# Pooled attention and a three-way maxout layer: more products by the seven-product scheme, and loads that wait for work ahead of them, in one written order

## The chip, the cores and the metric

The kernel runs on one core of a Trainium2 chip. The metric is the device time of one execution in microseconds (us); lower is better. TensorE is PE in the profile, its weight loads PEld, VectorE DVE, ScalarE ACT, GpSimd POOL, SyncE SP.

## The reference

```python
# q, k, v: (8, 8, 576, 64) float32: batch, heads, sequence, head size
k_p = k.reshape(B, H, 72, 8, D).mean(axis=3)       # keys and values pooled by 8
v_p = v.reshape(B, H, 72, 8, D).mean(axis=3)
scores = scale * np.matmul(q, k_p.transpose(0, 1, 3, 2))
attn = softmax(scores)
attn_out = np.matmul(attn, v_p)                    # (8, 8, 576, 64)
x = attn_out.transpose(0, 2, 1, 3).reshape(4608, 512)
h = np.maximum(np.maximum(x @ w1, x @ w2), x @ w3) # w1, w2, w3: (512, 768)
out = h @ w_out                                    # (768, 512)
```

## The kernel before

**Attention.** Eight batches, one after the other. Keys and values are loaded by POOL's queue as 16-bit numbers (load_k, load_v, load_q), 576 KB each, into two buffers a kind. The eight rows of a pool are added in three steps (fold_steps, L157 to L164): for batch 1 the keys on DVE, from batch 2 on keys and values on POOL. turn_k (L204) turns the pooled keys with TensorE and copies them with zeros into a block matrix kz; queries are turned by TensorE for batches 0 to 2 and by one DMA transpose on SP from batch 3 on (L302). scores (L227) gives a whole head at a time, 576 columns in two PSUM banks; from batch 7 on scores_flat (L234) gives pieces of 512 columns. ACT takes the exponential. values (L264) multiplies 128 tokens with the pooled values of eight heads and a column for the sum, DVE takes the reciprocal (rcp) and multiplies (xn). turn_x brings the tokens into xT, a ring of 2048 tokens with channels in partitions: by TensorE up to batch 2, by DMA transposes on SP (L253) from batch 3 on.

**Maxout.** With w2 - w1 and w3 - w1 in place of w2 and w3, the hidden layer is max(0, x(w2 - w1), x(w3 - w1)) plus x w1, and the output is that maximum times w_out plus x times wm, where wm = w1 w_out is made once (linear, L345). Tokens go in nine tiles of 512, numbered 0 to 8. An ordinary first layer (hidden, L362) takes 48 matmuls of 512 columns for a tile; an ordinary output (project, L412 and L416) takes 40 of 512 columns.

**Seven products.** A two by two block product can be made with seven block products instead of eight, when sums of the blocks are made first. The kernel uses this form with products named 1 to 7: PRODUCTS names the operands, S1 to S4 sums of the weight blocks and T1 to T4 sums of the token blocks. A first layer then takes 84 matmuls of 256 columns (seven, L789), an output 70 of 256 (out_seven, L713). Before, first layers of tiles 6, 7 and 8 are made so, and outputs of tiles 2, 3, 4, 7 and 8. Weight sums are made on DVE (fold_w L536, fold_out L597), token and hidden sums on DVE in tiles 2 to 4 (L612) and partly on POOL in tiles 6 to 8 (L564, L628).

**Order.** Every engine runs its instructions in the order in which the program gives them. Tile 0 and the start are run by block with a plan of steps in slots, tiles 1 to 4 by the lists in MIDDLE, tile 5 by LEAD, the rest by ORDER in weave. In MIDDLE a step such as `k5<` loads the keys of batch 5, and the key load waits for the last first-layer matmul issued before it; `!` makes the next POOL step wait for the last weight or token sum on DVE (gate). Stores of finished rows (osb, ob) go out on SP, 128 or 256 KB each.

Of the kernel before, what the change touches and what calls it, by code (L numbers as in the profile page):

```python
# [14 lines left out]
def kernel(  # L15
# [11 lines left out]
    nc = tc.nc  # L27
# [37 lines left out]
    kts, vts, qbs, kps, qTs, ets = {}, {}, {}, {}, {}, {}  # L65

# [15 lines left out]
    def load_v(b, eng, dtype=F16, cuts=(0, H)):  # L82
        if b == 0:
            vts[0] = ld.tile([96, 4096], dtype, name="vt0", tag="vt")[:, 0:3072].rearrange(
                "p (h i d) -> p h i d", h=H, i=6)
            src = v[0].rearrange("h (p i) d -> p h i d", i=6)
            return [eng.dma_start(out=vts[0][:, h:g], in_=src[:, h:g])
                    for h, g in zip(cuts, cuts[1:])][-1]
# [5 lines left out]
    def load_q(b):  # L94
# [4 lines left out]
        for i in range(0, 4, n):  # L99
            nc.gpsimd.dma_start(out=qbs[b][:, i:i + n], in_=src[:, i:i + n])  # L100
# [42 lines left out]
    vp_all = const.tile([Sp, B, H, 65], F16, name="vp", tag="vp")  # L143
# [10 lines left out]
    def fold(e, t, out, dtype=F32):  # L154
        return list(fold_steps(e, t, out, dtype))

    def fold_steps(e, t, out, dtype=F32):  # L157
        part, n = t.shape[:2]
        f = const.tile([part, n, 4, D], dtype, name="half" if dtype == F32 else "halfh",
                       tag="half" if dtype == F32 else "k16")  # L160
        yield e.tensor_tensor(out=f, in0=t[:, :, 0:4, :], in1=t[:, :, 4:8, :], op=ALU.add)  # L161
        yield e.tensor_tensor(out=f[:, :, 0:2, :], in0=f[:, :, 0:2, :],  # L162
                              in1=f[:, :, 2:4, :], op=ALU.add)
        yield e.tensor_tensor(out=out, in0=f[:, :, 0, :], in1=f[:, :, 1, :], op=ALU.add)  # L164

    def new_kp(b):
        kps[b] = sb2.tile([96, 6, D], BF16, name="kp", tag="kp")

    def fold_k(b, e, i0=0, i1=6):
        if b not in kps:  # L170
            new_kp(b)
        fold(e, kts[b][:, i0:i1], kps[b][:, i0:i1], F16 if e is nc.vector else F32)

    def fold_v(b):
        fold(nc.gpsimd, vts[b], vp_all[:, b, :, 0:D])

    def pool_v(b, h, g, tag, evac):

        pvp = psum([128, g - h, D], F32, name="pvp", tag=tag[0], bufs=tag[1])
        for i in range(6):  # L180
            nc.tensor.matmul(pvp, pick[:, i, :], vts[b][:, h:g, i, :],
                             start=(i == 0), stop=(i == 5))
        evac(out=vp_all[:, b, h:g, 0:D], in_=pvp[0:Sp])

    def turn_q(b, n0, n1, evac, tag):
# [5 lines left out]
        for n in range(n0, n1):  # L191
            nc.tensor.transpose(pqt[:, n - n0, :], qf[:, 128 * n:128 * n + 128],
                                ident)
        evac(out=qTs[b][:, n0:n1, :], in_=pqt)  # L194

    def keys(b, tag):
        pkt = psum([128, 3, 96], BF16, name="pkt", tag=tag[0], bufs=tag[1])
        for i in range(3):
            nc.tensor.transpose(pkt[:, i, :],
                                kps[b][:, 2 * i:2 * i + 2, :].rearrange("p i d -> p (i d)"),  # L200
                                ident[0:96, 0:96])
        return pkt

    def turn_k(b):  # L204
        pkt = keys(b, ATT if len(pools) < 3 else SC)
        for par, evac in enumerate((nc.vector.tensor_copy, nc.scalar.copy)):
            for odd in range(2):
                (evac if b > 2 else nc.vector.tensor_copy)(
# [4 lines left out]
    def score(b, h, out, tp, i0, i1):  # L213
# [4 lines left out]
        nc.tensor.matmul(out, kz_all[b % 2][f % 2][rows, h, :],  # L218
# [28 lines left out]
    def turn_x(b, c0, keep, xn, tag, evac=nc.scalar.copy):  # L247
        g0 = S * b + c0
        if b > 2:
            cut = 128 - (g0 + 128) % RING  # L250
            cuts = (keep, cut, 128) if keep < cut < 128 else (keep, 128)
            for a, z in zip(cuts, cuts[1:]):
                nc.sync.dma_start_transpose(  # L253
                    out=tokens(g0 + a, g0 + z),
                    in_=xn.rearrange("p g h d -> p (g h d)")[a:z])
            return
        pxt = psum([128, KCH, 128], F16, name="pxt", tag=tag[0], bufs=tag[1])
        for kc in range(KCH):
            nc.tensor.transpose(
# [4 lines left out]
    def values(b, c0):  # L264
        tag = (ATT0, ATT, ("val", 1))[len(pools) - 1]
        pav = psum([128, 2, 512], F32, name="pav", tag=tag[0], bufs=tag[1])
        for h in range(H):
            nc.tensor.matmul(  # L268
                pav[:, h // 4, 65 * (h % 4):65 * (h % 4) + 65],
                ets[b][:, h, c0:c0 + 128], vp_all[:, b, h, :],  # L270
# [18 lines left out]
    xns, mms = {}, []  # L289

    def do(b, steps):
# [3 lines left out]
        for name in steps.split():  # L295
            i = int(name[1:] or 0)
            if name[0] in "qQ":
                turn_q(b, *QS[i], nc.vector.tensor_copy if name[0] == "Q"
                       else nc.scalar.copy, TR)
# [680 lines left out]
```

## Time and profile before

| | us |
|---|---|
| median of three runs (lowest, highest) | 226.58 (226.14, 226.96) |
| the profiled execution | 228.01 |
| its span, first to last instruction | 226.3 |

| engine | busy us | share of the span | instructions |
|---|---|---|---|
| PE | 214.7 | 95% | 1807 |
| DVE | 148.6 | 66% | 292 |
| ACT | 122.3 | 54% | 221 |
| POOL | 138.6 | 61% | 111 |

The granted TensorE clock is 1.00 over the whole span. Busy times of DVE and ACT overlap where one instruction starts before the one ahead has ended, and a matmul's own duration runs past the start of the next one; work on TensorE is therefore better counted by the distance between two starts. The chain of waits names the work that ended last at each step; idle time of an engine that is not the bottleneck costs nothing.

### The profile page before, as it was taken

The page shows a single profiled execution, that of the slowest core. Times are in us where ns is not written, and L with a number is a line of the kernel's source. Part 1 is how long each engine was busy: PE and PEld are TensorE (multiplying, and loading weights), DVE is VectorE, ACT ScalarE, POOL GpSimd, SP SyncE. Part 2 cuts the span into 40 slices and gives each one's busy share as a digit, 9 for nine tenths or more (in the row PEclk, how much of TensorE's full clock was granted, in tenths as well). Part 3 has the DMA queues.
Part 4 walks back from the last instruction along what each step waited for, and adds up shares of the span by engine and source line. Part 5 has one row for each costly group of instructions (what it writes and reads, how often), then busy time and mean ns, then how long its engine had stood idle before and what let it go on. Part 6 is the DMA issues. An engine that isn't in the chain of part 4 may idle for free.

```text
span 226.3 us, 4691 instructions
## 1 busy us (share of the span) xinstructions
PE 214.7 (95%) x1807; PEld 146.4 (65%) x1807; DVE 148.6 (66%) x292; ACT 122.3 (54%) x221; POOL 138.6 (61%) x111
## 2 busy tenths in 40 slices
PE   6788999999999999999999999699999999999993
PEld 2467745558656555965686568355677677788882
DVE  3668876038595385876679668535668886898840
ACT  2267524755874577238624862475687446555330
POOL 7974300999949967787677758999500913872020
PEclk9999999999999999999999999999999999999999
DMA  6999999989759999659999599965241534200265
GB/s 167 210 197 197 208 207 208 203 163 224 128 106 191 217 220 208 112 129 151 199 226 191 31 216 236 182 126 132 58 107 29 122 61 95 46 3 0 55 203 164
DMA packets 47351, 33.54 MB, mean 148 GB/s; under 512 B 27041, under 2 KB 42337, under 8 KB 47329
## 3 DMA queue, kind: packets, MB, share of 16 engines
q0 software_dynamic: 16944, 16.98, 48.1%
q1 hardware_dynamic: 29936, 15.87, 33.0%
q10 hardware_dynamic: 448, 0.39, 0.7%
q8 instruction: 14, 0.23, 0.5%
q14 instruction: 9, 0.07, 0.1%
HBM read 34.60 MB, written 9.44 MB: 195 GB/s over the span
## 4 chain that ended last, share of the span: by engine, by line
PE 69%; DMA 15%; POOL 11%; issue 1%; DVE 1%; ACT 1%; POOLq 0%
PE pw L362 21%; PE oA L713 9%; DMA vt<-in_v_dram 8%; PE pA L789 7%; PE po L416 7%; PE po L412 5%; PE oC L713 4%; PE psc L218 4%; DMA mw<-in_moe_w_dram 4%; PE pC L789 3%; POOL half L161 3%; DMA xT<-xn 3%; PE pav L268 3%; PE oB L713 2%; POOL half L162 2%; PE pB L789 2%
## 5 line engine op out<-in xcount | busy, mean ns | idle before, releaser
L362 PE MATMUL pw<-xT,mw 128*128 128x512 f16 (+1 forms) x336 | 72.8, 348 | 1.9 <-DMA xT<-xn 1.6
L362 PEld LDWEIGHTS <-mw 128*128 128x128 f16 x336 | 31.6, 98 | 22.3 <-DMA xT<-xn 1.8
L370 DVE TENSOR_TENSOR hT<-t,pw 128x512 f16<-128x512 f16 (+1 forms) x42 | 25.4, 609 | 25.1 <-ACT et L223 17.8
L223 ACT ACTIVATE et<-psc 72x576 f16<-72x576 f32 (+2 forms) x54 | 35.2, 661 | 6.8 <-PE psc L218 6.7
L161 POOL TENSOR_TENSOR half<-vt 72x2048 f32<-72x2048 f16 x7 | 28.4, 4061 | 13.8 <-DMA vt<-in_v_dram 13.3
L162 POOL TENSOR_TENSOR half<-half 72x1024 f32<-72x1024 f32 (+1 forms) x13 | 27.3, 2098 | 11.0 <-DVE rcp L274 6.1
L368 ACT ACTIVATE t<-pw 128x512 f16<-128x512 f32 (+1 forms) x42 | 22.5, 537 | 16.2 <-PE pw L362 15.8
L276 DVE TENSOR_TENSOR xn<-pav,rcp 128x512 f16<-128x512 f32 x40 | 27.7, 692 | 1.4
L416 PE MATMUL po<-mwo,hT 128*128 128x512 f16 (+1 forms) x102 | 23.5, 366 | 0.0
L218 PE MATMUL psc<-qT,kz 128*128 128x320 bf16 (+2 forms) x120 | 22.4, 278 | 0.8 <-DVE qT L194 0.6
L218 PEld LDWEIGHTS <-kz 128*128 128x128 bf16 x143 | 13.1, 98 | 13.3 <-ACT qT L194 1.1
L161 POOL TENSOR_TENSOR half<-ktFalse 96x1536 f32<-96x1536 f16 x6 | 18.7, 3125 | 4.0 <-issue 2.9
L564 POOL TENSOR_TENSOR pad<-xT 128x256 f16<-128x256 f16 x8 | 5.9, 732 | 22.5 <-ACT pad L795 13.9
L795 ACT CAST pad<-pA 128x512 f16<-128x512 f32 x27 | 15.6, 588 | 7.2 <-PE pA L789 7.0
L268 PEld LDWEIGHTS <-et 72*128 72x128 f16 x320 | 15.1, 98 | 3.6 <-issue 0.4
L723 ACT COPY osb<-oA 128x512 f32<-128x512 f32 x12 | 7.0, 586 | 19.2 <-PE oA L713 19.2
L274 DVE RECIPROCAL rcp<-pav 128x8 f32<-128x8 f32 x40 | 8.2, 204 | 14.0 <-PE pav L268 13.6
L412 PE MATMUL po<-wm,xT 128*128 128x512 f16 (+1 forms) x68 | 16.6, 366 | 0.0
L268 PE MATMUL pav<-vp,et 72*128 72x65 f16 x320 | 16.4, 194 | 0.1
L421 ACT COPY osb<-po 128x512 f32<-128x512 f32 (+1 forms) x16 | 9.2, 573 | 12.0 <-PE po L416 12.0
L789 PEld LDWEIGHTS <-sw 128*128 128x128 f16 x144 | 13.7, 98 | 2.5
L766 DVE TENSOR_TENSOR pad<-pad,pC 128x512 f16<-128x512 f16 x18 | 12.3, 685 | 3.9 <-PE pC L789 3.6
(122 smaller groups left out, 380.0 us busy)
## 6 DMA issues: line engine op xcount, KB each, us to landing
out_dram<-osb SPq DMA_DIRECT2D x38, 128.0 KB, 5.5
ktFalse<-in_k_dram POOLq DMA_DIRECT2D x7, 576.0 KB, 8.2
qb<-in_q_dram POOLq DMA_DIRECT2D x7, 576.0 KB, 13.0
vt<-in_v_dram POOLq DMA_DIRECT2D x7, 576.0 KB, 17.5
mw<-in_moe_w_dram POOLq DMA_DIRECT2D x9, 256.0 KB, 9.4
out_dram<-osb SPq DMA_DIRECT2D x8, 256.0 KB, 7.4
ktTrue<-in_k_dram SPq DMA_DIRECT2D x3, 384.0 KB, 5.2
out_dram<-ob SPq DMA_DIRECT2D x8, 128.0 KB, 2.6
```

What stands on the lines that cost most here:

```text
L161: yield e.tensor_tensor(out=f, in0=t[:, :, 0:4, :], in1=t[:, :, 4:8, :], op=ALU.add)
L162: yield e.tensor_tensor(out=f[:, :, 0:2, :], in0=f[:, :, 0:2, :], in1=f[:, :, 2:4, :], op=ALU.add)
L218: nc.tensor.matmul(out, kz_all[b % 2][f % 2][rows, h, :], qTs[b][rows, n + i0:n + i1, 64 * (h % 2):64 * (h % 2) + 64], start=True, stop=True)
L223: nc.scalar.activation(out=out, in_=in_, func=FT.Exp, scale=1.0 / 64.0)
L268: nc.tensor.matmul(pav[:, h // 4, 65 * (h % 4):65 * (h % 4) + 65], ets[b][:, h, c0:c0 + 128], vp_all[:, b, h, :], start=True, stop=True)
L276: nc.vector.tensor_tensor(out=xn, in0=pv[:, :, :, 0:D], in1=rcp.to_broadcast([128, 2, 4, D]), op=ALU.mult)
L362: mm = nc.tensor.matmul(pw, w_sb[wi][:, kc, bass.ts(jc, 128)], x[:, kc], start=(kc == 0), stop=(kc == KCH - 1))
L370: nc.vector.tensor_tensor(out=hT[:, jc, c0:c1], in0=t, in1=pw, op=ALU.max)
L412: nc.tensor.matmul(po, tokens(128 * m, 128 * m + 128)[:, kc], wm_sb[:, kc, c], start=(kc == 0), stop=False)
L416: nc.tensor.matmul(po, hT[:, jc, bass.ts(mm, 128)], wo_sb[:, jc, c], start=False, stop=(jc == JCH - 1))
L713: nc.tensor.matmul(p, left, right, stop=(r == 4), skip_group_check=True, start=(i in FIRST and r == 0 and (m == 0 or n == LAST)))
L789: mm = nc.tensor.matmul(p[:, w], a[:, kc, bass.ts(g, 128)], b[:, kc, :], start=(i in FIRST and w + kc == 0), stop=(w + kc == 2), skip_grou ...
```

## The change

The start of the program, up to the first layer of tile 0 and the product wm, is the same. Behind it:

- Tile 5's first layer and the outputs of tiles 1, 5 and 6 are made by seven products too. Only tile 0's output is ordinary now (project), and tile 1's first layer is made in halves of 256 tokens.
- Product 1 is copied into the PSUM bank in which products 2 and 3 add up, so the sums with product 1 are made by TensorE. PSUM has four banks that are taken and given back in turn (take, give), two for scores and turns, and two for values.
- All scores from batch 1 on are scores_flat: 23 matmuls a batch instead of 16, and nine exponentials of 512 columns instead of eight of 576.
- The key sums go from POOL to DVE, in two steps instead of three; the third addition is made by TensorE, which turns both halves of the sum into one bank (keys). The copies of the turned keys are on ACT, but for batch 1. The value sums stay on POOL, in six pieces a batch (four of 512 columns, two of 512 columns); the last addition is on DVE.
- All weight, token and hidden sums are on DVE (both, sum_t, sum_h). Each value piece on POOL waits for the last of these sums that was issued before it.
- The query transposes on SP are made in three parts a batch. Every load waits for the last matmul issued before it and for the last DMA transpose issued before it.
- From tile 0's output on, one list (ORDER, run) gives the order of everything. `<k3` loads keys of batch 3, `K3` and `V3` are pieces of its sums, `k3` turns keys, `s30` to `s38` are scores, `v30` to `v34` values, `T3` transposes a third of the queries, `A1` to `H4` are ordinary first-layer products, `1a` to `7c` first-layer products of the seven, `1d` to `7d` output products, `t` and `u` sums of tokens and hidden rows, `f F S G` weight sums; a star puts the copy on DVE.

```diff
+    def matmul(*args, **kw):
+        latest[0] = nc.tensor.matmul(*args, **kw)
+        return latest[0]
...
+    def fold_k(b):
+        new_kp(b)
+        f = const.tile([96, 6, 4, D], F16, name="halfh", tag="k16")
+        nc.vector.tensor_tensor(out=f, in0=kts[b][:, :, 0:4, :], in1=kts[b][:, :, 4:8, :],
+                                op=ALU.add)
+        nc.vector.tensor_tensor(out=kps[b].rearrange("p j i d -> p i j d"), in0=f[:, :, 0:2, :], in1=f[:, :, 2:4, :],
+                                op=ALU.add)
...
         for i in range(3):
-            nc.tensor.transpose(pkt[:, i, :],
-                                kps[b][:, 2 * i:2 * i + 2, :].rearrange("p i d -> p (i d)"),
-                                ident[0:96, 0:96])
+            for j in range(2):
+                matmul(pkt[:, i, :], kps[b][:, j, 2 * i:2 * i + 2, :].rearrange("p i d -> p (i d)"),
+                                 identh[0:96, 0:96], start=(j == 0), stop=(j == 1))
...
-                qTs[b] = sb2.tile([128, 2 * NG, 128], BF16, name="qT", tag="qT")
-                nc.sync.dma_start_transpose(
-                    out=qTs[b], in_=qbs[b].rearrange("p hp t d -> p (hp t d)"))
+                if i == 0:
+                    qTs[b] = sb2.tile([128, 2 * NG, 128], BF16, name="qT", tag="qT")
+                turned[:] = [nc.sync.dma_start_transpose(
+                    out=qTs[b][:, 6 * i:6 * i + 6],
+                    in_=qbs[b].rearrange("p hp t d -> p (hp t d)")[:, 768 * i:768 * i + 768])]
...
+    def both(out, a, b, op, e=nc.vector):
+        t = e.tensor_tensor(out=out, in0=a, in1=b, op=op)
+        if e is nc.vector:
+            shared[:] = [t]
...
+    def sum_t(x, t, i):
+        a, b = ((x[1], x[0]), (x[3], t[:, 0]), (x[3], x[1]), (x[2], t[:, 1]))[i]
+        both(t[:, i], a, b, ALU.subtract)
...
+        if i == 1:
+            move(out=bank("B", n, g), in_=p)
+        elif i in (6, 5):
+            move(out=y[:, i == 5], in_=p)
+        elif i in (2, 3):
+            t0 = sb2.tile([128, NB], F16, name="t0", tag="t0")[:, 0:HALF]
+            nc.scalar.activation(out=t0, in_=p[:, 0], func=FT.Relu)
+            nc.vector.tensor_tensor(out=h_of(g)[:, i - 2], in0=t0, in1=p[:, 1], op=ALU.max)
...
+        for i in range(0, H, 2):
+            c = slice(i, i + 2)
+            yield e.tensor_tensor(out=f[:, c], in0=t[:, c, 0:4, :], in1=t[:, c, 4:8, :],
+                                  op=ALU.add)
+        for i in range(0, H, 4):
+            c = slice(i, i + 4)
+            yield e.tensor_tensor(out=t[:, c, 0:2, :], in0=f[:, c, 0:2, :], in1=f[:, c, 2:4, :],
+                                  op=ALU.add)
+        both(vp_all[:, b % 3, :, 0:D], t[:, :, 0, :], t[:, :, 1, :], ALU.add)
+        yield
+
+    def piece(what, b):
+        if (what, b) not in folding:
+            folding[what, b] = pieces(what, b)
+        gate = shared[0]
+        op = next(folding[what, b])
+        if op is not None and gate is not None:
+            after([op], gate)
...
+    SEVEN = (5, 6, 7, 8)
...
+            elif name[0] == "<":
+                load = {"k": load_k, "v": load_v, "q": load_q}[name[1]](
+                    int(name[2]), *([nc.gpsimd] if name[1] != "q" else []))
+                after([load], latest[0])
+                if turned:
+                    after([load], turned[0])
...
+    ORDER = """
+        V1 q12* q13 V1 p V1 V1 s10 s11 V1 p* <k3 F s12 s13 p s14 s15 p* K2 s16 s17 <k4 V1
+        <q3 V2 p s18 K2 q20* V1 k2 q21* V2 <v3 T3 p v10 s20 s21 p v11 s22 x10* p x11* V2 V2
+        q22 V2 v12 s23 C3 s24 q23* v13 V2 A3 V2 s25 K3 V3 s26 D3 s27 <q4 v14 s28 E3 G S K3
+        x13 V3 x12 H3 x14 v20 f B3 G D4 v21 S x20 k3 V3 A4 C4 x21 v22 s30 <v4 T3 H4 T3 S s31
+        t1 E4 x22 v23 s32 t2 G B4 s33 s34 K4 C1 K4 s35 V3 V3 u1 <k5 v24 s36 <q5 B1 s37 C2 F
+        k4 V3 t4 T4 f s38 A1 B2 x24 <k6 A2 u2 T4 x23 t1 V3 D1 T4 u4 s40 s41 V4 f V4 1d* V4
...
```

The last output tile (8) is made as before, by out_last, with its last two stores on SP.

739 lines of the change are left out of this document (322 added, 417 removed), and 3 rows, old and new, of the table stop.

## The prediction

> **What bounds the kernel now.** I read the page first, then the stretches by time, then the chain of work in order of time. The page gives each engine's share and the slices:
>
> ```profile
> PE 214.7 (95%) x1807; PEld 146.4 (65%) x1807; DVE 148.6 (66%) x292; ACT 122.3 (54%) x221; POOL 138.6 (61%) x111
> ...
> PE   6788999999999999999999999699999999999993
> ```
>
> TensorE (PE) is full in nearly every slice. Is it full of work or of stretched instructions? The chain shows pure TensorE runs, so the distance between starts can be read off:
>
> ```profile
> 78.72 2.59 PE pw L362 x12
> ...
> 92.89 1.09 PE oA L713 x10
> ...
> 138.71 6.32 DMA xT<-xn
> 145.17 1.02 PE pw L362 x4
> ```
>
> Twelve 512-column matmuls take 2.59 us, 216 ns each; ten 256-column ones 1.09 us, 109 ns each. The same distances between starts, taken over the trace, are 136 ns for 320 columns, 82 for 192, 56 for 128, 42 for 96, 33 for 65 and 28.5 for 64. Multiplied by the kernel's 1807 matmuls they give 208.55 us. The last matmul starts at 222.22 and the span ends at 226.30, so TensorE ahead of that start is 208.44 us of columns plus 13.78 us of waits. The waits lie as follows (real time less column time): 8.7 us up to 30 us, 1.6 from 30 to 60, 0.8 from 60 to 140, 2.6 around 140 to 150, 0.1 after. The end adds 4.08. So the kernel is bound by TensorE columns; waits after the start are 5 us in all, half of them the one place where turned tokens (xT) and turned keys come late:
>
> ```profile
> 142.19 0.29 PE L199 MATMUL pkt<-ident,kp 96*128 96x96 bf16 x3 [0.41 <-DVE rcp L274]
> ...
> 145.17 1.02 PE L362 MATMUL pw<-xT,mw 128*128 128x512 f16 x4 [1.59 <-DMA xT<-xn]
> ```
>
> Sums go against the profiled execution: 228.01 us, span 226.30. The median of the runs shown, 226.58, is 1.43 below it, and I carry the difference over unchanged.
>
> **The change, part by part.**
>
> *Columns.* The instruction lists give, before to after: 512 columns 431 to 249, 256 columns 801 to 1117, 320 columns 52 to 28, 192 columns 4 to 28, 128 columns 142 to 166, 96 columns 45 to 66, 64 columns 12 to 36, 65 columns 320 in both. By the distances: -39.3 +34.4 -3.3 +2.0 +1.3 +0.9 +0.7 = **-3.3 us**. Tile 5's first layer gives 1.2 of it (48 x 216 to 84 x 109 ns), the output products of tiles 1, 5 and 6 give 1.0 each (40 x 216 to 70 x 109). The flat scores of batches 1 to 6 (23 instead of 16 matmuls a batch) and the keys' two half sums (42 instead of 21) give some back. Against this part stands a rule of the Trainium skill, "TensorE: Matmul & The Clock Gate", section "Back-to-back issue gap": in a stream with weight loads 512 columns take about 131 ns and 128 columns about 81. By a line through those two, an estimate, a 256-column matmul takes 98 ns and the trade costs 7 us instead of saving. This trace does not agree: two 256-column matmuls cost 218 ns, one of 512 costs 216.
>
> *Start, 0 to 30 us.* The same instructions in the same order up to the first tile's last product: 8.7 us of waits stay.
>
> *30 to 60 us.* TensorE asks for batch 2's keys at 46.0. Load k2 landed at 45.1 in this trace and the loads ahead of it are unchanged; both key halves now run on VectorE (DVE), 0.95 and 0.55 us by the rows of batch 1, so they end near 46.8: a wait of 0.8. The four copies of the turned keys are then all on ScalarE (ACT), 4 x 0.48: another 0.3 at the first score. The new wait here: load k4 waits on GpSimd (POOL) for the first key half of batch 2, and behind it in POOL's queue stands the sixth value piece of batch 1, then load q3. Four pieces of 1.02 and two of 1.17 (quarters of 4.06, halves of 2.35) from the landing of v1 at 39.3, with two load issues of 0.55 and that wait, end at 48.1; the last add on DVE at 48.5; the first value product needs it at about 48.9. Hidden by 0.4; if k2 lands a microsecond later, it shows. Sum 1.5, before 1.6: **0**.
>
> *60 to 145 us.* The two waits of before (2.6) go: keys no longer pass through POOL, and loads are issued behind the transposes. What is late next? DVE. It gains six key folds (9.4), seven last value adds (2.4), 16 token sums (5.4), 14 hidden sums (6.6) and about 3 in copies: counted by distances between starts, 131.8 to 158.5 us. In the 75 us of TensorE time from 45 to 120 that is 64.9 us; in 105 to 120 alone it is 14.7 of 15. POOL loses 64 us (key folds 35.6, last value adds 8.9, sums 19), but its 42 value pieces stand between DVE's sums, and the trace shows what that does:
>
> ```profile
> 62.08 1.26 POOL L164 TENSOR_TENSOR vp<-half 72x512 f16<-72x512 f32 x1
> 62.28 1.35 DVE L597 TENSOR_TENSOR so<-wm 128x512 f16<-128x512 f16 x1
> ...
> 63.66 0.42 DVE L597 TENSOR_TENSOR so<-so,wm 128x512 f16<-128x512 f16 x1
> ```
>
> The DVE sum that began under a POOL add took 1.35 instead of 0.42: it ended 0.3 after POOL did. The change makes every value piece wait for the last such sum before it. Where the next sum stands directly behind, DVE has it running before POOL hears of the first; that is so in 11 of the 19 places from 45 to 120. At about five, 0.3 to 0.9 us of other DVE work lies between, and the next sum waits 0.2 to 0.8. So about 3 us of DVE waits against 10.1 us of room. Lower bound: 0.3 us of TensorE loss, only the hops between engines. Upper: all 19 wait 1.0, 19 - 10.1 = 9 us. I take 2.0, nearer the low end because most places are of the harmless kind; before had 3.4: **-1.4**.
>
> *Loads and transposes.* Turned queries are now three transposes a batch on SP. The first of batch 3 waits for q3; four stores of tile 0 stand behind it, and their buffers are next written near 85: nothing. q3 has k3 and k4 ahead of it, 2.9 us each after v2's landing at 48.6, and some 2 us of stores: it lands near 59.5. Scores of batch 3 start near 65.5. A whole transposed batch took 4.0, 7.0 at the median and 10.2 us at most to land in this trace; a third of it 1.3 to 3.4. Covered by 2.5. On POOL load q4 stands behind a value piece that waits for v3 (near 64), lands near 71, is needed near 80. Later loads have 10 us and more. **0**, bounded by 0 and the 4 of the second rival.
>
> *After 145.* TensorE lost nothing in 150 to 222 before; DVE's share there is 50 of 65 us and POOL does nothing: **0**.
>
> *End.* Before, the last copy was followed by two stores on two queues, landed 2.2 us after the first issue. Now the last add is followed by two 128 KB stores on SP alone; such a pair at 220.8 landed its second 3.2 after the first issue. **+1.0** (0.3 to 1.2).
>
> Sum: -3.3 + 0 - 1.4 + 0 + 1.0 = -3.7. Profiled execution 224.3, span 222.6; median **222.9**.
>
> **The rivals.**
>
> *Everything hides.* DVE keeps up as its room says, waits from 60 to 145 are 0.3 and the end adds 0.3: 2.4 us less, 220.5. For it: when the chain behind each TensorE wait is laid against column time, without queues, none is late by more than 0.5 us. Against: the kernel before lost more than such a count gives, too.
>
> *Transposes late.* If the first third of batch 3 or 4 takes the whole 7 us median or more, because load v3 or k5 and q5 share the DMA engines, TensorE stands 1.3 to 4.5 us: about 226. For: a transpose of before needed 10.2 with loads beside it. Against: the new loads are held back until earlier transposes are done.
>
> *Slower: DVE becomes the bound.* One mechanism, between 45 and 120 us: sums wait for POOL pieces. Each of the 19 places costs up to 1.0; room is 10.1; break-even with before comes when TensorE loses 5.7, that is at (10.1 + 5.7) / 19 = 0.83 a place. At 1.0: 9 us lost, 229.9. For: 105 to 120 has no room at all, and the queue is in order, so one late sum delays the release of the four product banks. Against: the 11 places above. The Trainium skill ("SBUF — State Buffer", section "Who interferes with whom") says that whoever issues first holds the shared port for the whole instruction and the other blocks; by that rule the order at each place decides, as I counted.
>
> *The saving is not there.* Matmuls of 256 columns slower than half of 512: only if the 98 ns weight load stopped being hidden under 109 ns. The trace has 801 of them at 109.
>
> **How the numbers follow.** Forecast (2.0, give or take 1.5 in the middle): 221.4 to 225.5, chance 0.50. Everything hides: 0.18. Transposes late: 0.12, about half of it within the no-change band. DVE bound: 0.17. Saving not there or something unseen: 0.03. A measurement of this kernel tells 0.3%, 0.7 us, from no change. Faster: 0.50 + 0.18 + 0.04 = 0.72; same 0.08; slower 0.20. The range leaves out the lowest of the second case and the worst of the DVE case: 220.2 to 228.0.
>
> **What would show it.** Right: 256-column matmuls still 109 ns apart; the slice of the old xT wait full; DVE busy near 175 us and POOL near 75; a wait under 1 us for the keys at 46; the last two stores on SP ending the span. Wrong: DVE sums of 0.8 to 1.4 us beside POOL pieces from 45 to 120, with TensorE idle behind DVE; scores of batch 3 or 4 waiting for qT; value products of batch 1 waiting for vp near 49; or any TensorE idle after 150.

## The result and the profile after

The changed kernel takes 234.69 us (median of four runs, 232.84 to 236.35) against 226.58 (226.14 to 226.96): 1.0332 times as long, 95% interval 1.0241 to 1.0422. The forecast was 222.9, range 220.2 to 228.0. The profiled execution is the shortest of the four, 232.84 us with a span of 230.8. Some executions of these kernels, of the one before too, come out some per cent longer than the rest; ratios are made without them, so a ratio can lie below the quotient of two medians, and no row is shown from a profiled execution that was such a one (runs 2, 3, 5, 12, 14 and 16).

The page of the changed kernel, shares and slices:

```profile
PE 213.8 (93%) x2009; PEld 163.1 (71%) x2010; DVE 172.7 (75%) x352; ACT 129.1 (56%) x256; POOL 83.4 (36%) x90
...
PE   7688999989999998899989996999999999999991
...
PEclk9999999999999999799999999999999999999999
```

DVE is at 172.7 us (the prediction wanted about 175), POOL at 83.4 (75). TensorE has slices of 6 and 8 in the middle of the span where it had 9s, and in one, the 17th (92 to 98 us), the granted clock fell. Column time, made as in the prediction, is now 205.1 us; one 512-column matmul of the start, near 10 us, has no record in this trace, and with it column time is 205.3. Real time less column time stands at 8.9 us at 30 (0.2 of it is the matmul without a record, here and in the next three figures), 11.0 at 60, 20.0 at 145 and 20.9 at the last matmul's start (225.82); behind that start come 5.0 us. Before it stood at 8.7, 10.3, 13.7 (at 150) and 13.8, with 4.1 behind. So the saving in columns is there, and the loss lies between 60 and 145 us: 9.0 us of waits instead of 3.4.

TensorE's timeline in that stretch has four waits worth the name (start, length, operation; in brackets the idle time before it and what ended it):

```profile
93.47 0.50 PE L70 MATMUL pav<-vp,et 72*128 72x65 f16 x8 [2.14 <-DVE xn L277]
93.78 1.04 PE L70 MATMUL pb<-xT,mw 128*128 128x512 f16 x2
...
107.03 0.27 PE L70 MATMUL psf<-qT,kz 128*128 128x256 bf16 x1 [0.33 <-DMA qT<-qb]
...
119.91 0.54 PE L70 MATMUL psf<-qT,kz 128*128 128x320 bf16 x4 [0.98 <-DMA qT<-qb]
...
141.75 0.60 PE L70 MATMUL pb<-sums,xT 128*128 128x256 f16 x4 [2.01 <-ACT osb L78]
```

Two are scores waiting for turned queries. The old wait on xT at 145, 1.59 us before, is gone. After 93.47 there is more than the wait: two 512-column matmuls take 1.04 us, and the next ones start 427 ns apart instead of 216, up to 97.3 us; that half clock costs another 1.7 us. By the distances between starts, which come out 0.16 us above the idle times in brackets, the 9.0 us are 1.6 at 107 and 120, 2.2 at 142, 4.0 at 93 with the half clock behind it, 0.6 at 66 (a wait on xn), and 0.6 in smaller pieces.

*Behind 107 and 120: transposes beside a load.* The chain of work in order of time, and POOL's and SP's own rows:

```profile
98.62 8.37 DMA qT<-qb
...
112.84 7.03 DMA qT<-qb
...
122.45 11.56 DMA qb<-in_q_dram
```

```profile
99.38 0.79 POOL L112 DMA_DIRECT2D qb<-in_q_dram  x1 [0.47 <-PE pb L70]
...
112.71 0.54 POOL L92 DMA_DIRECT2D ktFalse<-in_k_dram  x1 [6.01 <-PE pb L70]
121.61 0.85 POOL L104 DMA_DIRECT2D vt<-in_v_dram  x1 [8.36 <-DMA xT<-xn]
```

```profile
111.56 5.10 SPq L303 DMA_TRANSPOSE qT<-qb  x3
```

The third part of batch 5's transpose, issued at 98.62, landed at 106.98; the load of q6, issued at 99.38, landed at 106.65. The second part of batch 6's, issued at 112.84, landed at 119.86; load k7, issued at 112.71, at 119.11. The first part of batch 6's, issued at 111.56, 1.1 us ahead of that load, took 2.8 us, and the second of batch 5's, issued 2.1 us ahead of q6's load, 4.0. So in these two batches a part that went out beside a load, or less than a microsecond ahead of it, landed about when the load did; a part with more of a lead did not.

*Behind 142: SP stands.* Load q7 went out at 122.45, held up in POOL's queue by load v6, which had waited 8.4 us for transposes, and landed at 134.02. SP, in order, had reached batch 7's transposes at 125 and stood with seven stores behind; ScalarE then waited 5.75 us for the buffers of those stores:

```profile
134.04 2.54 SPq L303 DMA_TRANSPOSE qT<-qb  x2
136.69 4.91 SPq L690 DMA_DIRECT2D out_dram<-osb  x7
141.11 0.59 ACT L78 COPY osb<-pb 128x512 f32<-128x512 f32 x1 [5.75 <-DMA out_dram<-osb]
```

*Behind 93: values in DVE's order.* DVE's and POOL's rows:

```profile
75.17 1.19 DVE L535 TENSOR_TENSOR sums<-mw 128x768 f16<-128x768 f16 x1
...
76.62 2.33 DVE L535 TENSOR_TENSOR sw<-mw 128x768 f16<-128x768 f16 x1
...
92.15 0.42 DVE L535 TENSOR_TENSOR vp<-vt 72x512 f16<-72x512 f16 x1 [2.77 <-POOL vt L809]
```

```profile
74.69 1.26 POOL L809 TENSOR_TENSOR vt<-half 72x512 f16<-72x512 f32 x1
...
77.25 1.28 POOL L809 TENSOR_TENSOR vt<-half 72x512 f16<-72x512 f32 x1
...
81.89 6.90 POOL L805 TENSOR_TENSOR half<-vt 72x512 f32<-72x512 f16 x4 [2.87 <-issue]
```

Of two weight sums of 0.55 us, one took 1.19 beside a POOL addition and the next 2.33 while POOL issued load q5 and added another piece (to 78.5). POOL's next piece was gated on a DVE sum behind that one and began at 81.89; four pieces of batch 4 took 6.90 (pieces average 1.28 us over the run, forecast 1.02), load v5 and two more followed, DVE's last value add waited 2.77 us for them, and batch 3's values stood behind it in DVE's queue. TensorE needed those at 91.3.

*Why it is so tight.* The first scores of batches 4, 5 and 6, before and after:

```profile
102.87 0.41 PE L218 MATMUL psc<-qT,kz 128*128 128x320 bf16 x2
...
124.58 0.41 PE L218 MATMUL psc<-qT,kz 128*128 128x320 bf16 x2
...
146.03 0.41 PE L218 MATMUL psc<-qT,kz 128*128 128x320 bf16 x2
```

```profile
78.93 0.60 PE L70 MATMUL psf<-qT,kz 128*128 128x320 bf16 x5
...
102.69 0.60 PE L70 MATMUL psf<-qT,kz 128*128 128x320 bf16 x5
...
117.18 0.60 PE L70 MATMUL psf<-qT,kz 128*128 128x320 bf16 x5
```

| batch | query load issued, before / after | landed | first scores | last part of turned queries landed |
|---|---|---|---|---|
| 4 | 66.27 / 64.38 | 72.00 / 72.04 | 102.87 / 78.93 | 86.81 / 80.20 |
| 5 | 79.44 / 76.43 | 90.37 / 84.85 | 124.58 / 102.69 | 105.94 / 106.98 |
| 6 | 101.15 / 99.38 | 112.48 / 106.65 | 146.03 / 117.18 | 124.14 / 120.53 |

The new order brings the scores of these batches forward by 22 to 29 us; their query loads go out only 2 to 3 us earlier, and the first of their transposes 3 to 6. Before, turned queries lay ready 16 to 22 us ahead of the first scores. Now their last parts land 1 to 4 us after the first scores have begun.

### The profile page after: what moved, and what is told of

It reads as the page before. It is cut to its first block, busy times and chain, and to the rows that moved or that the text cites. A ratio compares the mean times of both kernels' runs of the same rounds, so it can differ in the third digit from the quotient of the medians.

```text
span 230.8 us, 5153 instructions
## 1 busy us (share of the span) xinstructions
PE 213.8 (93%) x2009; PEld 163.1 (71%) x2010; DVE 172.7 (75%) x352; ACT 129.1 (56%) x256; POOL 83.4 (36%) x90
## 4 chain that ended last, share of the span: by engine, by line
PE 60%; DMA 17%; DVE 6%; POOL 5%; issue 5%; SPq 3%; ACT 2%; POOLq 0%; ACTq 0%
PE pb L70 43%; DMA qT<-qb 7%; DMA qb<-in_q_dram 5%; PE psf L70 4%; PE pw L70 4%; DMA vt<-in_v_dram 4%; PE pav L70 3%; SPq L303 2%; PE pm L70 2%; DVE xn L277 2%; POOL vt L809 2%; POOL half L805 2%; DMA out_dram<-osb 1%; PE pxt L74 1%; PE oC L70 1%
## 5 line engine op out<-in xcount | busy, mean ns | idle before, releaser
L70 PE MATMUL pb<-xT,mw 128*128 128x256 f16 (+1 forms) x336 | 62.7, 321 | 0.2 <-DVE hT L644 0.2
L805 POOL TENSOR_TENSOR half<-vt 72x512 f32<-72x512 f16 x28 | 35.5, 1283 | 46.6 <-DMA vt<-in_v_dram 24.5
L224 ACT ACTIVATE et<-psf 72x512 f16<-72x512 f32 x63 | 34.8, 589 | 9.4 <-PE psf L70 9.3
L70 PE MATMUL psf<-qT,kz 128*128 128x256 bf16 (+4 forms) x161 | 22.2, 249 | 1.7 <-DMA qT<-qb 1.3
L680 DVE TENSOR_TENSOR hT<-t,pb 128x512 f16<-128x512 f16 (+1 forms) x30 | 17.1, 576 | 7.3 <-PE pb L70 3.8
L70 PEld LDWEIGHTS <-hs 128*128 128x128 f16 x192 | 18.8, 98 | 2.2
L70 PEld LDWEIGHTS <-hT 128*128 128x128 f16 x168 | 16.6, 99 | 3.8
L70 PE MATMUL pb<-mwo,hT 128*128 128x256 f16 (+1 forms) x120 | 19.3, 294 | 0.0
L70 PE MATMUL pb<-soh,hs 128*128 128x256 f16 x138 | 19.1, 273 | 0.0
L78 ACT COPY pb<-pb 128x512 f32<-128x512 f32 x18 | 10.3, 572 | 15.8 <-PE pb L70 15.1
L809 POOL TENSOR_TENSOR vt<-half 72x512 f16<-72x512 f32 x14 | 17.7, 1278 | 2.2 <-DVE xs L535 2.2
```

What stands on the lines that cost most here:

```text
L70: latest[0] = nc.tensor.matmul(*args, **kw)
L78: (nc.vector.tensor_copy if on_vector[0] else nc.scalar.copy)(out=out, in_=in_)
L224: nc.scalar.activation(out=out, in_=in_, func=FT.Exp, scale=1.0 / 64.0)
L680: nc.vector.tensor_tensor(out=hTs[n][:, j, c], in0=relus[j], in1=b, op=ALU.max)
L805: yield e.tensor_tensor(out=f[:, c], in0=t[:, c, 0:4, :], in1=t[:, c, 4:8, :], op=ALU.add)
L809: yield e.tensor_tensor(out=t[:, c, 0:2, :], in0=f[:, c, 0:2, :], in1=f[:, c, 2:4, :], op=ALU.add)
```

## Experiments

Theory after the result: the transposes of queries have lost their slack, and a load beside them, SP's queue or DVE's order decides by a microsecond who waits. Rivals: the loads' added waits are the cost; the gate of POOL's pieces is; DVE is the bound. Ratios are to the kernel before in the same series; the changed kernel's own is 1.033.

**1. Loads without their waits.**

```diff
-                after([load], latest[0])
-                if turned:
-                    after([load], turned[0])
```

> Changed kernel, but the loads no longer wait for the matmul and the transposes issued before them; only buffers hold them back. In the changed kernel POOL stood 6.0 us for a matmul (load k7) and 8.4 us for a transpose (load v6), q7 landed at 134.0, SP stood for it with seven stores behind, and TensorE lost 2.2 us at 141.7. Theory 'load waits': q7 lands before 120, the loss at 141.7 goes and so do parts of 107 and 120: 2 to 4 us less than the changed kernel's 233 to 236, about 230.5. Rival 'contention': loads now run beside the transposes, turned queries and tokens land later than their median, TensorE waits for qT or xT by 2 us or more somewhere between 60 and 110, and the total is the same or up to 4 us longer.

246.15 us, ratio 1.0839 (1.0765 to 1.0913). TensorE stands for turned queries:

```profile
131.97 1.01 PE L70 MATMUL psf<-qT,kz 128*128 128x320 bf16 x5 [9.87 <-DMA qT<-qb]
```

The added waits, taken together, are not the cost. In this order they save 11 us.

**2. Value pieces without their gate** (the `after([op], gate)` in piece taken out).

> Changed kernel, but POOL's value pieces no longer wait for the last DVE sum issued before them. Theory 'port': POOL and DVE block each other around 75 to 89 in any order; without the wait POOL starts earlier, more DVE sums of 0.5 us stretch to 1.0 to 1.5, but the value pieces of batch 4 end 3 us earlier, so the 2.3 us wait at 93.5 and the half clock behind it (1.6) go: about 4 us less, near 230. Rival 'the wait protects DVE': DVE sums are stretched at more places than the eight of the changed kernel, DVE busy grows from 172.7 by 5 us or more and the total by 1 to 4 us.

244.75 us; no ratio, as runs scattered from 237.30 to 248.41. Its lowest run lies above the highest of the changed kernel's four (236.35), though run 16 below has that kernel once at 239.40. So the gate seems to help too; by how much and in what way this run does not show.

**3 and 4. One move each.** Batch 7's three transposes moved behind `k7 s68 D2 B2`; batch 4's last value add, which is DVE's, moved behind `3d*`.

> Changed kernel, but the three query transposes of batch 7 are issued on SP some 15 us later in the order, behind the stores of the output tile that followed them. Theory 'order on SP': the 5.8 us for which ACT waits on a store, and TensorE's 2.2 us at 141.7, go; nothing else moves: 2 us less, about 232. Rival 'DMA': the stores are late because the DMA engines are busy with loads v6, q7 and v7 up to 137; then the wait at 141.7 stays within 0.7 us of 2.2.

> Changed kernel, but the last value add of batch 4 stands later in DVE's order, behind the fourth group of value products of batch 3 instead of ahead of the second. Theory 'order on DVE': DVE waited 2.8 us there for POOL with the division of the value products behind it, TensorE stood 2.3 us at 93.5 and then ran at half clock for 3.2 us (1.6 lost); all of it goes: 3.9 us less, about 230 to 231, granted clock 1.00 over the span. Rival 'port': DVE is late there anyhow from sums held by POOL around 75 to 79, and the wait at 93.5 shrinks by less than 1 us.

233.07 us, 1.0278 (1.0239 to 1.0317), and 234.25, 1.0352 (1.0267 to 1.0437): neither told apart from 1.0332. What the first move did to the wait at 142 is left open. In the second the wait at 93 shrank to 0.6 at 90 and 0.4 at 98, as wanted, and the loss stood up at batch 6's turned queries:

```profile
121.78 0.91 PE L70 MATMUL psf<-qT,kz 128*128 128x320 bf16 x4 [4.84 <-DMA qT<-qb]
```

The second part of batch 6's transpose was issued at 112.00 and landed at 121.73; load k7 ran from 111.80 to 120.98. So in this run the loss at 120 grew by about what the loss at 93 shrank.

**5 and 6. Loads behind the transposes, first tries.** Load k7 behind batch 6's third part; then that, q6 behind batch 5's third part, and moves 3 and 4.

```diff
-        s50 s51 V5 E2 s52 V5 <k7 v41 s53 T6 T6 D1 D2 s54 T6 ...
+        s50 s51 V5 E2 s52 V5 v41 s53 T6 T6 D1 D2 s54 T6 <k7 ...
```

> Only the load of batch 7's keys moves: behind the third part of batch 6's query transpose instead of ahead of the first, so that by the rule of the changed kernel it now waits for that part to land. Theory 1 (a part of a transpose that is under way when a load is issued lands with that load: 112.84 to 119.86 us beside the key load's 112.71 to 119.11; 113.81 to 123.59 beside 114.16 to 123.62 in the run with batch 7's transposes moved): the second and third part land 2 to 4 us after their issue, the wait of scores on qT near 120 us (1.1 us in the profile of the changed kernel, 4.3 and 5.0 in the two runs with one move each) goes, and the time falls by 1 to 5 us, to 228 to 233 us. Theory 2 (the transposes are late because their queries came late, 106.65 us, or because SP stood): the parts land as late as they did and the time stays within 1 us of 234.7. Theory 3 (what the load loses comes back: the key load lands 4 to 6 us later, keys and values of batch 7 wait): the wait at 120 goes and another of 2 us or more stands up between 125 and 145 us.

> Four moves in the order at once, nothing else: the load of batch 7's keys behind the last part of batch 6's query transpose, the load of batch 6's queries behind the last part of batch 5's, batch 7's three parts to just ahead of its scores' last neighbours as in the run with that move, and the last piece of batch 4's values late as in the run with that move. If the losses after 60 us are loads that overtake query transposes, a queue that stands, and values in VectorE's order, each by itself, then all go: of 11.2 us that TensorE lost after 60 us by waits and half clock, the 0.5 at 107, 1.1 at 120, 2.2 at 142 and some 3.5 of the 3.9 at 93 go, and the time is 226 to 229 us. If a loss only moves on to the next buffer or queue (as it did after each move alone), a new wait of over 2 us appears and the time stays at 231 to 234 us.

240.37 us (235.87 to 241.59), for which there is no ratio, and 234.21, 1.0353 (1.0306 to 1.0401). In the second, batch 6's parts landed 2.8 to 4.2 us after issue and no score waits at 107 or 120; new waits on xn (1.9 at 126) and on batch 7's queries (3.5 at 146) took their place. Run 5's theory 1 is right on the transposes: moving the loads alone made the parts land in time. The expected gain is wrong: the loss moved on.

**7. No value pieces on POOL** (six of seven left out for batches 1 to 7, so the output is not the reference's).

> GpSimd's value pieces of batches 1 to 7 are left out (six of the seven pieces each, with their waits on VectorE's sums), so the values are wrong; GpSimd only issues loads. If VectorE's sums are held by GpSimd's pieces (2.33 us for a weight sum of 0.55, 1.19 for another) and its last value add by the pieces not being done (2.77 us at 92), then VectorE's busy time falls from 172.7 to 165 us or less, the waits on xn at 66 and 93 us go (2.9 us, with the half clock after the second 4.5), and the time falls by 4 to 6 us if the query transposes stay as they are. If the transposes are the main loss and VectorE has room, its busy time may fall but the time stays within 2 us of 234.7, with waits on qT of 2 us or more between 100 and 125 us.

239.80 us, 1.0592 (1.0572 to 1.0611). DVE's rows became what was expected: busy 168.2 us instead of 172.7, every weight sum of 768 columns 0.55, and no wait on xn at 66 or 93. But POOL's loads, k5 and q5, now went out at 73.05 and 73.58, and batch 4's third part, issued at 73.38, landed at 87.32:

```profile
87.36 0.37 PE L70 MATMUL psf<-qT,kz 128*128 128x256 bf16 x1 [4.61 <-DMA qT<-qb]
```

With DVE's trouble gone the kernel is slower, because loads go out at other times and turned queries come later still. So DVE alone does not bound it; what DVE's part costs in the changed kernel, this run cannot price.

**8. Loads that wait for the matmul only.**

> Of the two added waits of a load, that on the transposes ahead of it is taken out; that on the matmul ahead of it stays. If it is the wait on transposes that keeps loads off them, this run stands near the one with both waits out (246 us), with waits of scores on qT of 3 us or more. If the matmul's wait alone already times the loads, it stays within 2 us of 234.7. In between (237 to 243 us) both have a part.

245.81 us, 1.0857 (1.0778 to 1.0935), as slow as without both waits, and one wait says why:

```profile
129.59 0.64 PE L70 MATMUL psf<-qT,kz 128*128 128x320 bf16 x3 [12.12 <-DMA qT<-qb]
```

It is the wait on the transposes that saves the 11 us: the wait on the matmul alone saves next to nothing here.

**9. No query transposes for batches 4 to 7.**

```diff
+                if b > 3:
+                    qTs[b] = qTs[3]
+                    continue
```

> The query transposes of batches 4 to 7 are left out, and the scores of these batches use batch 3's queries, so the output is not the reference's. Nothing on TensorE waits for a query transpose after batch 3, SP has twelve transposes fewer to issue and the loads twelve fewer to wait for. If the transposes, placed 0 to 3 us ahead of their scores where the kernel before has 15 us and more, are the main loss, the waits on qT (1.6 us in the profile of the changed kernel, 4 to 6 us in the runs with one move) and the stand of SP at 134 to 141 us (2.2 us) go and the time falls from 234.7 to 227 to 230 us, with a spread of its runs of less than 2 us. If the main loss lies in VectorE and GpSimd (xn at 66 and 93 us), the time stays at 231 us or more.

230.05 us (228.30 to 230.72), 1.0176 (1.0158 to 1.0195): 4.6 less, the largest gain of any edit, and at the upper end of the 227 to 230 that were expected if the transposes are the main loss. From 60 to 145 TensorE loses 4.8 us instead of 9.0, and the one wait on qT left is batch 3's, which kept its transposes (1.2 us; the changed kernel's profile has no wait there). The edit takes more away than waits on qT: the loads that waited for these transposes are freed too, and the wait at 93 is gone as well, while the one on xn near 66 grew from 0.4 us to 1.6. So 4.6 us is the price of the transposes with all that hangs on them:

```profile
66.98 0.40 PE L74 MATMUL pxt<-identh,xn 128*128 128x128 f16 x4 [1.63 <-DVE xn L277]
73.14 0.27 PE L70 MATMUL psf<-qT,kz 128*128 128x256 bf16 x1 [1.20 <-DMA qT<-qb]
```

**10. One whole transpose a batch.**

> One transpose of a batch's queries at the place of its first part, as in the kernel before, instead of three parts. If the three issues a batch are what fills SP's queue between 96 and 125 us, the whole ones land earlier (one issue of 2 to 2.8 us instead of 4.6 to 5) and the time falls by 1 to 3 us. If what counts is the load that is under way with them, a whole transpose lands as late as the last part does, the first scores of a batch now wait for all of it, and the time stays or rises by 1 to 5 us, with single waits on qT of 3 us and more.

234.32 us, 1.0346 (1.0313 to 1.0379): no change. One wait of 3.15 us at 118.47 takes the place of two. SP was done with batch 6's whole transpose in 2.80 us, from 109.69, where the three parts took it 5.10 from 111.56; it landed at 118.43 all the same, beside load k7 (111.86 to 121.11). The number of issues on SP is not the matter.

**11 and 12. TensorE turns the queries of batches 5 and 6**; then with moves 3 and 4.

```diff
+                if b in (5, 6):
+                    turn_q(b, 6 * i, 6 * i + 6, move, SC)
+                    continue
```

> Batches 5 and 6 have their queries turned by TensorE at the places of the three parts (36 transposes of 128 columns at 56 ns by the distances of the trace, 2.0 us of TensorE time, and six copies out by ScalarE); the other batches stay. If the transposes by DMA are the loss there, the waits on qT at 107 and 120 us (1.6 us, and up to 5 us in other runs) go for 2.0 us of work: 231 to 234 us, with less spread. The wait at 142 us (2.2 us) stays or shrinks, as SP has six issues fewer. If TensorE then waits for the queries' loads themselves or for ScalarE's copies, there are new waits at the transposes of 1 us and more and the time stays at 234 us or above.

> The same with batch 7's three parts issued later and the last piece of batch 4's values later, as in the two runs with these moves. If each loss goes by itself (2.2 at 142, about 3 of the 3.9 at 93, qT at 107 and 120 for 2.0 of work), 227 to 230 us. If losses move on to the next wait, 231 us or more with a new wait of 2 us.

232.28 us, 1.0283 (1.0213 to 1.0353), and 233.76, 1.0216 (1.0192 to 1.0239; it rests on two of four runs, 230.97 and 231.61 us). The first is not told apart from 1.0332, though its time came out as expected; the second is the only edit that computes the same and whose interval lies below that of the changed kernel (1.0241 to 1.0422), and only just. In the first, profiled in its slowest run (235.04), TensorE now waits for the query load itself:

```profile
106.88 1.35 PE L74 MATMUL pqt<-ident,qb 128*128 128x128 bf16 x11 [3.42 <-DMA qb<-in_q_dram]
```

q6 landed just ahead of it. Even with no transpose in between, the order asks for these queries too early.

**13 to 16. SP's queue, all loads, both, and the changed kernel again.** Stores of the seven-product tiles on ScalarE (`store(nc.scalar, ...)` in two places); loads v4, q4, k5, q5, k6, q6 and k7 behind the last part of the transpose of their time (seven loads; the expectation counts eight).

> The stores of the seven-product tiles are issued by ScalarE instead of SP (two places in the code); nothing else. If SP's queue makes batch 6's transposes late (queries landed at 106.65 us, transposes issued from 111.56), they are issued from about 107 us, land by 111 to 114 us and the wait on qT near 120 goes; the wait of ScalarE for osb at 142 (its stores stood behind batch 7's transposes) goes too: 3.3 us less, 230 to 232 us. If ScalarE then waits for VectorE's sums that its stores need, TensorE gets new waits on ScalarE's copies (et, pb, kz) of 1 us and more, and the time stays at 234 us or above. If the loads alone decide, the waits on qT stay (1 to 5 us) and only the 2.2 at 142 goes: 232.5 us.

> Eight loads of batches 4 to 7 (queries 4, 5 and 6, keys 5, 6 and 7, values 4; keys 6 were behind already in part) stand behind the last part of the query transpose of their time, so that they wait for it to land. If a load under way is what makes transposes late, no part lands later than 4 us after its issue unless another load runs, the waits on qT at 70 to 78, 107 and 120 us go, and the time falls by 2 to 4 us, to 231 to 233 us. If the loads themselves become late by it (each 2 to 4 us later than before and one behind the other), keys, values or queries are waited for: kp, xn or qT waits of 2 us and more after 85 us, and 234 us or above.

> Both edits: stores on ScalarE and loads behind the transposes. If the two are the two halves of the loss, the time is 228 to 230 us (the run without the transposes of batches 4 to 7 gave 230.05); if losses move on, 232 us or more.

> The changed kernel once more, unedited. If its waits are fixed by the order, the profile shows the same four losses after 60 us at the same places (0.6 at 66, 2.3 at 93, 0.5 and 1.1 at 107 and 120, 2.2 at 142) within half a microsecond. If it depends on which load runs beside which transpose, and that on a microsecond either way, other waits on qT stand in the place of some (70 to 78 us, or 3 us and more at 120), and the sum of the losses differs by 2 us and more, as the times of its runs do (232.84 to 236.35).

283.74, 237.58, 277.06 and 233.95 us; ratios 1.2523 (1.2460 to 1.2585), 1.0341 (1.0256 to 1.0426), 1.2203 (1.2148 to 1.2258) and 1.0297 (1.0243 to 1.0352). The stores hold up ScalarE's own queue, and TensorE waits for ScalarE:

```profile
118.20 1.87 PE L70 MATMUL pb<-xT,mw 128*128 128x512 f16 x4 [11.41 <-ACT t L678]
```

ScalarE's queue rows there give 13.84 us for six store issues, and the releasers that they name are transposes of tokens and queries. So 13 and 15 tell nothing of SP; whether fewer stores ahead of the transposes would help stays open. Run 14 is not told apart from the changed kernel either: moving the loads behind the transposes does not bring the 2 to 4 us that were expected. The time of the changed kernel came back (233.95 beside 234.69); whether its waits stand at fixed places is not settled.

**17 and 18. Everything by the order alone.** As 14, with batch 7's transposes and key sums and batch 4's last value add late; then the same with k7's load and sums at their old places.

> As the run with eight loads behind the transposes, and three moves for the waits that it left: batch 7's transposes late (4.3 us at 146: SP stood with the stores behind), batch 7's key sums late (2.9 at 128: VectorE's first key sum waited for the keys, values behind it), batch 4's last value piece late (2.1 at 90). Of the 14.0 us between the offset at 60 (10.8) and its half clock and the one at 160 (27.2, without 2 us of half clock) some 9 go: 229 to 231 us, and slower than the kernel before by 1 to 2%. If losses only move on, 233 us or more, with a new wait of over 2 us. Faster than the kernel before (under 226) is expected by neither: the waits on xn at 66 (1.4) and on turned inputs at 100 (1.1) stay.

> The same with the load of batch 7's keys and its sums at their old places. If that load makes batch 6's transposes late, a wait on qT of 1 to 7 us stands near 120 us and the time is 1 to 5 us above the run with it moved; if the two are within 1 us, it was one load among several and the time lies elsewhere.

235.66 us (231.67 to 238.96), 1.0257 (1.0174 to 1.0339), and 236.22, 1.0439 (1.0394 to 1.0483). The first one's trace, of its run of 231.67 us, has no wait on turned queries over 0.31. What stands instead:

```profile
90.47 0.43 PE L70 MATMUL pav<-vp,et 72*128 72x65 f16 x8 [2.32 <-DVE xn L277]
...
99.64 0.59 PE L70 MATMUL pb<-xT,mw 128*128 128x512 f16 x2 [0.89 <-DMA xT<-xn]
...
128.35 0.43 PE L70 MATMUL pkt<-identh,kp 96*128 96x96 f16 x6 [2.05 <-DVE kp L535]
```

The first is values in DVE's order again, the second turned tokens, and the third is my own move: batch 7's key sums, put later, began at 126.76 though the keys had landed at 124.48, because DVE was full from 123.5. With the keys' load where it was (18), batch 6's third part took 6.9 us to land beside it and 4.1 without it (17), but no score of that batch waited for it; batch 7's did, 4.06 us at 145.54. The intervals of 17 and 18 lie apart, by some 4 us between the runs that they rest on (231.67 and 233.20 against 235.44 to 237.25), so k7's place with its sums counts, but not through the wait near 120 that was expected. No version beat the kernel before. The best by the time, at 230.05, is the one without transposes, which computes with other queries; of those that compute the same, run 12 has the lowest ratio.

## Why the prediction failed, step by step

**Right.** Columns: with the matmul that has no record, 205.3 us by the same distances against 208.55, -3.3 as said; ten 256-column matmuls still stand 109 ns apart and 512-column ones 216, so the 131 ns of the Trainium skill ("TensorE: Matmul & The Clock Gate", "Back-to-back issue gap") does not hold here either. Start: 8.7 us, that matmul taken off, against 8.7. Keys of batch 2: 0.95 for 0.8 said. End: 5.0 us behind the last matmul's start, 5.1 said. The old wait on xT is gone. Four stores behind batch 3's first part: no wait followed.

**A little off.** Values of batch 1, "hidden by 0.4", showed 0.26. 30 to 60 lost 2.0 for 1.5. After 145: 0.9 for 0.1. The stretch from 60 to 145 lost 9.0 for 2.0; that is 7.0 us of the miss, and two terms share it.

**The step that failed: loads and transposes, "Later loads have 10 us and more. 0".** The first clause was true and the conclusion false. From q6's landing to its scores are 10.5 us (106.65 to 117.18). In these the transposes stood 4.9 us in SP's queue (first issue 111.56), then a load went out beside them and they needed 7.0. I had worked out the wait of batches 3 and 4 only, and had not held the new place of the scores against the old: 22 to 29 us earlier with loads that start only 2 to 3 us earlier. A size was wrong as well: I gave a third of a batch a third of a whole transpose's time to land, 1.3 to 3.4 us. The 15 parts of the changed kernel took 2.7 to 8.4, and 12 of them more than 3.4. The term I set to 0 is 3.8 us in the profiled execution: 1.6 at 107 and 120, and 2.2 at 142, where SP stood. I found stores behind transposes harmless at batch 3 and did not look at batch 7. By run 9 (medians 234.69 and 230.05) it is 4.6, above my bound of 4, with the caveat given there: that run also changes when loads go out and what DVE waits for.

**The second term, 60 to 145 "2.0" for DVE.** In the profiled execution the waits on xn at 66 and 93, with the half clock, come to 4.6 us. Without those transposes (run 9) the stretch loses 4.8 us, of which 1.4 are batch 3's turned queries; that leaves 3.4. Both lie inside the bounds of 0.3 and 9, at about twice my value. The rows bear out the first half of my mechanism: between 45 and 120 us five sums on DVE were held beside POOL (at 63.67, 65.94, 75.17, 76.62 and 101.11), 3.4 us beyond their usual lengths, for about five places and 3 us said. The 32 hidden sums kept 0.55 us. What I had wrong is the way from there to TensorE. I set the 3 us against 10.1 us of room on DVE; but late sums hold back POOL's gated pieces, the last value adds then waited 4.2 us for POOL, and the values that TensorE needs stood behind them in DVE's queue:

```profile
L535 DVE TENSOR_TENSOR vp<-vt 72x512 f16<-72x512 f16 x7 | 2.9, 420 | 4.2 <-POOL vt L809 4.2
L535 DVE TENSOR_TENSOR sw<-mw 128x768 f16<-128x768 f16 x2 | 2.9, 1437 | 0.0
```

Both the waiting and the long sums go when POOL's adds go (run 7). The Trainium skill's rule of the shared port ("SBUF — State Buffer", section "Who interferes with whom": whoever issues first blocks the other) agrees with the sum at 75.17, which began under a POOL addition and ended 0.4 us after it. It does not by itself explain the one at 76.62, which began 0.6 us ahead of the addition at 77.25, with a load being issued on POOL, and still ended 0.4 us after it. The half clock behind the wait at 93, 1.7 us, was in no term.

**The rivals.** "Transposes late" was the right mechanism with the wrong place and price: not the first thirds of batches 3 or 4 but the later parts of 5 and 6, with SP's stand at batch 7, and 3.8 to 4.6 us on top of all else instead of 226 in all. Its argument against itself, that loads are held back, holds as far as it goes (11 us more without, runs 1 and 8), but a load waits for the transposes ahead of it in the list, not for those behind. "DVE becomes the bound" gave the nearest time, 229.9, by luck: it wanted 1.0 us at each of 19 places, and five sums were held, for 3.4 us in all.

**The median.** I carried over that the profiled execution of before lay 1.43 us above the median. That of the changed kernel lies 1.85 below. Of the 11.8 us that the forecast missed, 8.5 are in the sum (232.84 for 224.3) and 3.3 here.

## What to carry to other kernels

When an order is rewritten, list for every transfer the time from its landing to its first reader, before and after, over the whole kernel: work that is moved earlier needs its loads moved too. Here 16 to 22 us of slack hid queues, transfers that slow each other and stretched sums alike; with the slack gone each of them shows, and taking one out let the next show (runs 4, 6 and 17). That giving the slack back would give the time back is argued, not shown: no run moved the loads earlier or the scores later. A rule that holds a load back until transposes are done guards only the transposes that stand ahead of the load in the order. Putting more loads behind them made parts land in 2.8 to 4.2 us (run 6), but it did not make the kernel faster.

## What the hardware showed that was not expected

A part of a query transpose (a third of a batch) lands later the more loads run beside it. In ten traces (the changed kernel and runs 1, 4, 6, 7, 8, 9, 11, 17 and 18), counting loads that overlap a part by more than a microsecond, 40 parts with none landed 2.7 to 5.1 us after issue (median 3.1), 56 with one 2.8 to 9.7 (median 4.5), and 36 with two or more 4.6 to 16.9 (median 7.3). A part that is late for another reason also meets more loads, so this count alone proves no cause; the runs that moved one load do (6.9 us beside k7 in run 18, 4.1 without it in run 17). The Trainium skill ("DMA: Bandwidth & Descriptors", section "Issuing engines are not separate DMA queues") has DMAs of all engines interleave on the same 16 engines; the rows agree with that, and the price here is a factor of two at the medians and five at worst.

The granted clock fell to half after some waits of TensorE and not after others of the same length. A wait of 2.14 us at 93.47 in the changed kernel was followed by 3.4 us at half clock, and so was one of 2.14 at 94.07 in run 8; the same wait at 93.24 in run 10 was not, nor were 2.32 and 2.05 us in run 17 and 2.01 at 141.75 in the changed kernel. Of two waits of 3.15 us, that at 118.47 in run 10 was followed by it and that at 125.64 in run 7 was not. The eight waits of 3.3 us and more in runs 1, 4, 6, 7, 8, 11 and 18 all were. The Trainium skill ("TensorE: Matmul & The Clock Gate", section "What's actually happening") gives an idle window of about 3.4 us that runs free and does not start with the wait. That equal waits end differently agrees with a window that runs free; a wait of 2.14 us that brings half clock is shorter than the window, so there the measurement decides.
